# Sliding-window attention with a dropless expert layer on one core: when the first expert tiles are closed, and which engine issues which load and store

## The chip, the cores and the metric

The kernel runs on one core of one Trainium2 chip. The metric is the device time of one execution in microseconds (us). Engines are called by their names (TensorE for matrix products, VectorE, ScalarE, GpSimd, SyncE); in the profile's rows they are PE (PEld its weight loads), DVE, ACT, POOL and SP. SPq, ACTq and POOLq are instructions with which those engines issue transfers.

## What is computed

Attention over 8 batch items with 8 heads, 576 positions and head width 64; a position sees itself and the 63 before it. Its output, 4608 tokens of 512 values, goes through a layer of 8 experts, of which each token takes the one with the largest logit.

```python
scores = scale * np.matmul(q, k.transpose(0, 1, 3, 2))
rel = pos[:, None] - pos[None, :]
mask = (rel >= 0) & (rel < 64)
scores = np.where(mask, scores, -1000000000.0)
attn = softmax(scores); out = np.matmul(attn, v)
x = out.transpose(0, 2, 1, 3).reshape(4608, 512)
logits = x @ w_gate                       # 512 x 8
expert_idx = np.argmax(logits, axis=1)
gate_w = softmax(logits)[np.arange(N), expert_idx]
for e in range(8):                        # tokens sorted by expert
    y[e's] = np.maximum(x[e's] @ w1[e], 0.0) @ w2[e]   # 512 x 1024, 1024 x 512
out = gate_w[:, None] * y
```

## The kernel before

**Attention.** Two batch items form a pair (`bg`, 0 to 3) of 1152 tokens, nine blocks of 128 (`NTB`): four whole ones of each item, and a ninth made of the last 64 positions of both (the "rests"). A unit `u` is a pair and two heads; there are 16. Each unit takes three steps (`c` = 0, 1, 2) of three blocks, so there are N = 48 steps, all written out; `step(s)` (L896) issues, in this order for every engine: `scored(s + 1)` (L550, q times k, into banks 0 and 1), `masked` (L578, VectorE) and `softened` (L591, exponentials on ScalarE); `weighted(s - 1)` (L609, times v, into bank 6); `logit(s - 3)` (L648); `flipped(s)` (L598, transposes of the weights; one copy back by VectorE, one by ScalarE); `divided(s - 1)` (L624, VectorE reads bank 6); loads, if the step is a unit's first; `turned(s + 3)` (L522, transposes of q and k, copied back by ScalarE; `c` = 2 turns the rests); `x_turned(s - 2)` (L637); and what stands under `s` in the dictionary `todo`. Each engine does its instructions in the order in which they are written. Before step 0, steps -3 to -1 run their parts: `turned(0)`, `turned(1)`, then `scored(0)` and `turned(2)`.

**Loads.** `load_qk(u)` (L481) issues eight loads of 128 KB for a unit, `load_v(u)` (L505) four, with GpSimd's copies that shift v by half a block; `load_rests(bg)` (L492) six for a pair. All are issued by SyncE, the first ones in the order of L876 to L883: unit 0's q and k, the gate weights `wg`, a zero row, the rests, v, then units 1 and 2.

**Routing.** When a pair's logits are complete, `by_tokens` (L661) and `choose` (L677) find on VectorE each token's expert, its gate weight and its rank among the expert's tokens, in five parts. `after` (L833) spreads them and what follows over the next steps: `place` (L744, two VectorE instructions a block), `weigh` (L751, x times gate weight) and `store` (L759, to `x_dram`).

**Expert tiles.** A tile has 256 slots, in two chunks of 128 tokens (`C` = 2). Tiles 0 and 1 always belong to expert 0 and hold tokens of the first three pairs only, so that they can start before the last pair is routed: after the third pair (`last - 1`), L730 raises expert 0's count to at least 512. `first_tiles` (L857), in the last part of `after` for that pair, writes the tokens of both tiles into `perm_e`: a comparison on VectorE (`hi_e`) and 54 small matmuls (L869). `gather_first` (L277) clears tile 0's rows and fetches them by an indirect load. A tile's work is `hidden` (L314, seven products of a Strassen-like scheme, each some 1.9 us of TensorE in the rows), `turn` (L299, transposes of the next tile, eight, with two copies by ScalarE), `sums_x` (L307, VectorE) and `output` (L367, seven more products). `sums_w2` (L152) forms four sums of w2 on GpSimd.

**Between.** After the last step the code from L939 on interleaves by hand the last attention parts, tile 0 (`next(tile0)` issues one product) and the last pair's routing, whose nine blocks ScalarE weighs in `weigh_some` and SyncE stores. `slot_table` (L779) then makes the table of all other tiles: a comparison (`hi`), `fill` for the first 27 blocks, `place` and `fill` for the last nine. Then come tile 1, expert 0's third tile, and a loop over the experts with branches on the counts (from L1007 on).

Of the kernel before, what the change touches and what calls it, by code (L numbers as in the profile page):

```python
# [20 lines left out]
WINDOW = 64  # L21
# [15 lines left out]
def kernel(  # L37
# [45 lines left out]
    ident = consts.tile([P, P], F32, name="ident")  # L83
    make_identity(nc, ident[:])
    GE = 32
    wg = consts.tile([P, NG, GE], F32, name="wg")
# [125 lines left out]
    key = rt.tile([P, NJE], BF16, name="key")  # L212
    hi_e = rt.tile([P, NJE, NE * C], BF16, name="hi_e")
    at_b = rt.tile([P, NJ], BF16, name="at_b")
# [21 lines left out]
    VW = D + 1  # L236
    ST = 3
    NST = NTB // ST
# [37 lines left out]

    def gather_first(tokens):  # L277

        for c in range(C):
            G.memset(xg[c], 0.0)  # L280

            G.indirect_dma_start(
                out=xg[c], out_offset=None, in_=x_dram[0 : NT - BG * S, :],
                in_offset=bass.IndirectOffsetOnAxis(ap=tokens[:, c : c + 1], axis=0),
                bounds_check=NT - BG * S - 1, oob_is_err=False,
            )
# [11 lines left out]

    def turn():  # L299

        for c in range(C):
            for g in range(NG):
                nc.tensor.transpose(out=tps[c][:, g, :], in_=xg[c][:, g * P : (g + 1) * P], identity=ident[:])  # L303
            nc.scalar.copy(out=xq[:, :, c], in_=tps[c].rearrange("p (a g) s -> p a g s", a=2))
        yield

    def sums_x():  # L307

        b12, b22, b21 = tps[1][:, 0:HG], tps[1][:, HG:], tps[0][:, HG:]
        for n, (a, b) in enumerate(((b12, xq[:, 0, 0]), (b22, xs[:, 0]), (b22, xq[:, 0, 1]), (xs[:, 1], b21))):  # L310
            V.tensor_tensor(out=xs[:, n], in0=a, in1=b, op=ALU.subtract)
# [128 lines left out]
    with tc.manual_schedule(), ExitStack() as held, ExitStack() as brief:  # L440
# [5 lines left out]
        sc_ring, tr_ring = cycle((0, 1)), cycle((2, 3, 4, 5))  # L446


        NM = 2 + ST
        mask = consts.tile([P, NM, P], BF16, name="mask")  # L450
        nc.gpsimd.memset(mask[:], 0.0)
        for h in range(2):
            for m0, m1, first in ((0, 1, False), (1, 2, h == 0), (2, NM, False)):
                rows = slice(h * D, (h + 1) * D)
                sel = partial(
                    nc.gpsimd.affine_select, out=mask[rows, m0:m1, :], in_=mask[rows, m0:m1, :], fill=MASKED,
                )
                if first:
                    sel(pattern=[[0, m1 - m0], [-1, P]], compare_op=ALU.is_ge, base=0, channel_multiplier=1)
                else:  # L460
                    sel(pattern=[[0, m1 - m0], [1, P]], compare_op=ALU.is_gt, base=0, channel_multiplier=-1)
                    sel(pattern=[[0, m1 - m0], [-1, P]], compare_op=ALU.is_ge, base=WINDOW, channel_multiplier=1)
        NVR = 3
# [16 lines left out]

        def load_qk(u):  # L481
            bg, g = units[u]
            qks[u] = [qk_m(((u % 3 + 2) % 3 * 2 + n) * 1024, BG, NV, 2, D) for n in range(2)]
            for i in range(BG):
                for t, src in zip(qks[u], (q, k)):
                    for h in range(2):
                        nc.sync.dma_start(
                            out=t[:, i, :, h, :],
                            in_=src[bg * BG + i, 2 * g + h, 0:SM, :].rearrange("(p j) d -> p j d", j=NV),
                        )  # L490

        def load_rests(bg):  # L492

            at = 6144 + bg % 2 * 2048
            vr = qk_m(at + 1024, BG, H, D)
            rests[bg] = [qk_m(at, H, D), qk_m(at + 512, H, D), vr]
            for t, src in zip(rests[bg], (q, k)):
                for i in range(BG):
                    nc.sync.dma_start(
                        out=t[i * D : (i + 1) * D], in_=src[bg * BG + i, :, SM:S, :].rearrange("h p d -> p h d")  # L500
                    )
            for i in range(BG):
                nc.sync.dma_start(out=vr[D:P, i], in_=v[bg * BG + i, :, SM:S, :].rearrange("h p d -> p h d"))

# [172 lines left out]
        def choose(bg):  # L677
# [49 lines left out]
            V.tensor_tensor(out=count[:], in0=count[:], in1=inc[:, :, NTB - 1], op=ALU.add)  # L727
            if bg == last - 1:

                V.tensor_scalar_max(count[:, 0:1], count[:, 0:1], float(NE * TB))  # L730
            V.tensor_tensor(out=rank[:], in0=rank[:], in1=ranks[:, 1], op=ALU.subtract)
# [47 lines left out]
        def slot_table(hi):  # L779
# [25 lines left out]
            def fill(j):  # L805
                for i in range(2):
                    nc.tensor.matmul(slots, lhsT=lo[:, i, j], rhs=hi[:, j], start=(i + j == 0), stop=(i + j == NJ))

            for j in range(NJE):
                fill(j)  # L810
            for n in range(NST):
                for m in range(ST):
                    place(NJE + n * ST + m)
                yield
            for j in range(NJE, NJ):
# [17 lines left out]
        def after(s, routing, bg):  # L833
# [13 lines left out]

            for n in (0, 0, 1, 2, 2):
                do(n, part)
            for m in range(NTB):  # L850
                do(3 + m // 3, partial(place, bg * NTB + m))
                do((2, 2, 3, 3, 4, 4, 4, 5, 5)[m], partial(weigh, bg, m, nc.scalar if m in (2, 6) else G))
                if m % ST == ST - 1:
                    do(3 + m // ST, partial(store, bg, m // ST, G))
            do(6, first_tiles)

        def first_tiles():  # L857

            V.scalar_tensor_tensor(
                out=key[:], in0=rkhi[:, 0:NJE], scalar=1.0, in1=oh_all[:, 0, 0:NJE], op0=ALU.add, op1=ALU.mult  # L860
            )
            V.tensor_tensor(
                out=hi_e[:], in0=_inner(key[:], NE * C), in1=_ins(hi_id[:, C + 1 : C + 1 + NE * C], 1, NJE),
                op=ALU.is_equal,
            )
            slots = banks[next(tr_ring)](0, NE * C)
            for j in range(NJE):
                for i in range(2):
                    nc.tensor.matmul(  # L869
                        slots, lhsT=lo[:, i, j], rhs=hi_e[:, j], start=(i + j == 0), stop=(i + j == NJE)  # L870
                    )
            V.tensor_scalar(out=perm_e[:], in0=slots, scalar1=-1.0, scalar2=float(NT), op0=ALU.mult, op1=ALU.add)
            gather_first(perm_e[:, 0:C])

        N = NU * NST
        load_qk(0)  # L876
        nc.sync.dma_start(out=wg[:, :, 0:E], in_=moe_w_gate.rearrange("(g p) e -> p g e", p=P))
        nc.sync.dma_start(out=x_dram[NT : NT + 1, :], in_=zrow[:])
        load_rests(0)
        load_v(0)  # L880
        load_qk(1)
        load_v(1)
        load_qk(2)  # L883

# [11 lines left out]
        def step(s):  # L896
            if 0 <= s + 1 < N:
                prs[s + 1] = softened(*masked(s + 1, scored(s + 1)))
# [7 lines left out]
            if s >= 0 and s % NST == 0:  # L906
                u = s // NST
                if u + 3 < NU and (u + 3) % NG == 0:
                    load_rests((u + 3) // NG)
                if u + 2 < NU:  # L910
                    load_v(u + 2)
                if u + 3 < NU:
                    load_qk(u + 3)
            if s + 3 < N:
# [13 lines left out]

        for n, s in enumerate((N - 6, N - 3)):
            fs = slice(n * HF, (n + 1) * HF)  # L930
            todo.setdefault(s, []).append(partial(nc.sync.dma_start, out=w2s[0][:, fs], in_=w2v[0][:, fs]))
        for s in range(-3, N):
            step(s)
        assert not todo
        sums_w2(0)

        tr_ring = cycle((4, 5))  # L939
        tile0 = chain(hidden(0), turn(), output(0))  # L940
        px = weighted(N - 1, pTs.pop(N - 1))
        form_all(turn())
        logit(N - 3)
        divided(N - 1, px)
        x_turned(N - 2)
        sums_x()
        gather_first(perm_e[:, C : 2 * C])
        by_tok = [by_tokens(last, c) for c in range(NST)]
        next(by_tok[0])
        next(tile0)  # L950
        logit(N - 2)
        x_turned(N - 1)
        next(by_tok[0], None)
        next(by_tok[1])
# [21 lines left out]
        weigh_some(1)  # L976
        next(tile0)
        next(routing, None)
        weigh_some(2)
        next(tile0)  # L980
        brief.close()
        hi = held.enter_context(tc.tile_pool(name="hot", bufs=1)).tile([P, NJ, NS], BF16, name="hi")
        table = slot_table(hi)
        for _ in range(8):
            next(tile0)
            next(table, None)
        assert next(tile0, None) is None
        gather(perm_i[:, 3 * C : 4 * C])
# [82 lines left out]
```

## Time and profile before

| | us |
|---|---|
| median of 3 runs (lowest, highest) | 765.39 (765.24, 767.0) |
| the profiled execution | 764.28 |
| its span, first to last instruction | 762.4 |
| TensorE busy | 720.1 (94%) |
| VectorE busy | 395.0 (52%) |
| GpSimd busy | 357.1 (47%) |
| ScalarE busy | 268.4 (35%) |
| mean granted TensorE clock | 0.986 |

Attention takes the first 214 us, tile 0 lasts until about 247 and tile 1 until about 275; the rest are the experts' other tiles. In the profile's rows the first number is the start, the second the duration, in us from the start of the span; then engine, line, operation, output <- inputs, shapes and number. In brackets stands how long the engine sat idle before, and what released it.

### The profile page before, as it was taken

The page shows a single profiled execution, that of the slowest core. Times are in us where ns is not written, and L with a number is a line of the kernel's source. Part 1 is how long each engine was busy: PE and PEld are TensorE (multiplying, and loading weights), DVE is VectorE, ACT ScalarE, POOL GpSimd, SP SyncE. Part 2 cuts the span into 40 slices and gives each one's busy share as a digit, 9 for nine tenths or more (in the row PEclk, how much of TensorE's full clock was granted, in tenths as well). Part 3 has the DMA queues.
Part 4 walks back from the last instruction along what each step waited for, and adds up shares of the span by engine and source line. Part 5 has one row for each costly group of instructions (what it writes and reads, how often), then busy time and mean ns, then how long its engine had stood idle before and what let it go on. Part 6 is the DMA issues. An engine that isn't in the chain of part 4 may idle for free. (4 is left out here: it accounts for less than half of the span.)

```text
span 762.4 us, 18401 instructions
## 1 busy us (share of the span) xinstructions
PE 720.1 (94%) x7018; PEld 650.5 (85%) x7018; DVE 395.0 (52%) x1355; ACT 268.4 (35%) x676; POOL 357.1 (47%) x366
## 2 busy tenths in 40 slices
PE   4999999999899999999999999999999999999995
PEld 3888888887688988998999899899988899988994
DVE  2677997988758544523542353352434452424432
ACT  4888888887543201211121122011220121211220
POOL 5215558593860635537531653663266465262111
PEclk8999999999899999999999999999999999999998
DMA  8997889983513712604410360542171171101101
GB/s 162 226 205 173 175 181 255 213 225 113 195 42 126 277 58 67 229 29 138 159 56 30 96 208 30 166 142 70 31 257 45 40 254 56 43 24 42 43 29 54
DMA packets 137620, 94.55 MB, mean 124 GB/s; under 512 B 117072, under 2 KB 117072, under 8 KB 137490
## 3 DMA queue, kind: packets, MB, share of 16 engines
q1 hardware_dynamic: 127858, 62.16, 29.8%
q0 software_dynamic: 9056, 28.58, 11.7%
q10 hardware_dynamic: 576, 2.10, 0.8%
q8 instruction: 78, 1.28, 0.7%
q14 instruction: 52, 0.43, 0.2%
HBM read 73.94 MB, written 20.45 MB: 124 GB/s over the span
## 5 line engine op out<-in xcount | busy, mean ns | idle before, releaser
L322 PE MATMUL bank<-qk_m,s 128*128 128x128 f32 x1216 | 145.4, 275 | 0.0
L322 PEld LDWEIGHTS bank<-qk_m,s 128*128 128x128 f32 x1216 | 140.4, 192 | 0.0
L322 PE MATMUL bank<-qk_m,w 128*128 128x128 f32 x912 | 112.2, 276 | 12.5 <-DVE v_m L358 8.8
L272 POOL DMA_INDIRECT qk_m<-x_dram,at_g x42 | 44.6, 1063 | 167.5 <-PE bank L303 160.2
L322 PEld LDWEIGHTS bank<-qk_m,w 128*128 128x128 f32 x912 | 106.7, 192 | 17.5 <-issue 17.3
L595 ACT ACTIVATE pr<-pr,mx 128x128 f32<-128x128 f32 x288 | 89.7, 390 | 31.8 <-DVE mx L585 31.5
L358 DVE TENSOR_TENSOR v_m<-bank,v_m 128x256 f32<-128x256 f32 x101 | 40.8, 422 | 110.1 <-PE bank L362 54.8
L585 DVE CUSTOM_DVE_ANT_0 pr<-bank,mask 128x128 f32<-128x128 f32 x288 | 64.4, 286 | 27.7 <-PE bank L572 26.1
L329 ACT COPY qk_m<-bank 128x512 f32<-128x512 f32 x19 | 11.2, 587 | 165.7 <-PE bank L322 155.2
L292 POOL DMA_INDIRECT out_dram<-v_m,at_s x42 | 42.4, 1010 | 56.5 <-DVE v_m L358 44.7
L139 POOL TENSOR_TENSOR s<-w 128x1024 f32<-128x1024 f32 x22 | 52.3, 2376 | 19.1 <-DMA qk_m<-x_dram,at_g 14.8
L362 PE MATMUL bank<-qkT_m,v_m 128*128 128x256 f32 x240 | 54.0, 380 | 1.7 <-DVE v_m L139 1.7
L362 PEld LDWEIGHTS bank<-qkT_m,v_m 128*128 128x128 f32 x240 | 45.4, 190 | 8.5 <-DVE v_m L139 2.5
L362 PE MATMUL bank<-qk_m 128*128 128x256 f32 x224 | 52.1, 380 | 0.0
L513 POOL COPY v_m<-v_m 64x520 f32<-64x520 f32 x32 | 19.8, 618 | 67.0 <-DMA v_m<-in_v_dram 59.7
L618 PEld LDWEIGHTS bank<-v_m,pT 128*64 128x64 f32 x1152 | 40.5, 139 | 11.6 <-DVE xs L632 5.8
L618 PE MATMUL bank<-v_m,pT 128*64 128x65 f32 x1152 | 47.2, 229 | 2.6 <-DVE xs L632 2.6
L362 PE MATMUL bank<-s,v_m 128*128 128x256 f32 x216 | 48.1, 379 | 0.0
L362 PEld LDWEIGHTS bank<-qk_m 128*128 128x128 f32 x224 | 41.5, 190 | 5.5 <-ACT v_m L374 0.4
L362 PEld LDWEIGHTS bank<-s,v_m 128*128 128x128 f32 x216 | 41.0, 190 | 5.6
L572 PE MATMUL bank<-qkT_m 64*64 64x128 f32 x1152 | 44.8, 286 | 0.1
L539 PE MATMUL bank<-ident,qk_m 128*128 128x128 f32 x256 | 36.6, 287 | 8.7 <-DMA qk_m<-in_q_dram 8.1
(167 smaller groups left out, 1220.7 us busy)
## 6 DMA issues: line engine op xcount, KB each, us to landing
w<-in_moe_w_dram SPq DMA_DIRECT2D x11, 2048.0 KB, 9.2
qk_m<-in_q_dram SPq DMA_DIRECT2D x72, 128.0 KB, 3.8
qk_m<-in_k_dram SPq DMA_DIRECT2D x72, 128.0 KB, 3.7
v_m<-in_v_dram SPq DMA_DIRECT2D x64, 128.0 KB, 3.7
qk_m<-in_moe_w_dram SPq DMA_DIRECT2D x3, 2048.0 KB, 16.1
x_dram<-xs POOLq DMA_DIRECT2D x6, 512.0 KB, 4.8
x_dram<-xs POOLq DMA_DIRECT2D x3, 768.0 KB, 5.3
w<-in_moe_w_dram ACTq DMA_DIRECT2D x4, 512.0 KB, 5.0
```

The costliest lines, as they stand in the source:

```text
L139: op()
L272: G.indirect_dma_start(out=xg[c], out_offset=None, in_=x_dram[:, :], in_offset=bass.IndirectOffsetOnAxis(ap=at_g[:, c : c + 1], axis=0),)
L292: put = G.indirect_dma_start(out=out[:, :], out_offset=bass.IndirectOffsetOnAxis(ap=at_s[:, c : c + 1], axis=0), in_=ys[c], in_offset=None ...
L322: nc.tensor.matmul(acc[:, f, :], lhsT=a[:, g, f * P : (f + 1) * P], rhs=b[:, g, :], start=(first and f == 0 and g == 0), stop=(g == HG - 1 ...
L358: plus = lambda out, a, b: V.tensor_tensor(out=out, in0=a, in1=b, op=ALU.add)
L362: nc.tensor.matmul(acc, lhsT=a[:, f, :], rhs=b[:, f, :], start=(start and f == 0), stop=(stop and f == HF - 1), skip_group_check=True,)
L513: nc.gpsimd.tensor_copy(out=vb[0:D, i].rearrange("p j h d -> p (j h d)"), in_=va[D:P, i].rearrange("p j h d -> p (j h d)"),)
L539: nc.tensor.transpose(out=tr.rearrange("d a b -> d (a b)").rearrange("d (p j) -> d j p", j=NV)[:, j, :], in_=t[:, c, j].rearrange("p h d - ...
L572: nc.tensor.matmul(out_, lhsT=qT[rows, t, a * WINDOW : (a + 1) * WINDOW], rhs=rhs, start=True, stop=True, skip_group_check=True,)
L585: V.tensor_tensor_reduce(out=prs[h][:, m, :], in0=scs[h][:, m, :], in1=mask[:, m0 + m, :], scale=-scale, scalar=-2 * MASKED, op0=ALU.add, ...
L595: nc.scalar.activation(out=y, in_=y, func=AF.Exp, scale=-1.0, bias=mx[:, h, m : m + 1])
L618: nc.tensor.matmul(px[a * D : (a + 1) * D, h, m, :], lhsT=pTs[h][:, m, a * D : (a + 1) * D], rhs=vt[:, h, :], start=True, stop=True, skip_ ...
```

## The change

- Expert 0's count is raised to 256 after the second pair and to 512 after the third. Tile 0 is filled from the first two pairs and tile 1 from the first three, each by its own `first_tile`: comparison first, then the small matmuls (36 for tile 0, 54 for tile 1, two columns wide instead of four) and the gather. Tile 0's comparison stands in step N-10, its matmuls and gather in N-9; tile 1's behind the last step.
- Tile 0's transposes and `sums_x` move into step N-2 (into banks 0 and 1), its first product and `sums_w2` into step N-1; the loads of w2 one step earlier.
- For the third pair, `choose`, `place` and `weigh` get other steps; GpSimd weighs all nine blocks (before: seven, ScalarE two), and SyncE stores instead of GpSimd.
- In the table, the fill of 27 blocks comes after the second three of the last places, and the last `weigh_some` comes later.
- The masks are made first on GpSimd. The rests of the first two heads are loaded by ScalarE, followed by the gate weights; v and unit 1 follow unit 0 directly on SyncE; the other heads' rests are loaded by GpSimd.
- `scored(0)` stands between `turned(0)` and `turned(1)`; ScalarE's exponentials for it come after `turned(1)`'s copies, and `turned(2)` comes in step 0.

The core of the diff (the move of the mask code, with its text unchanged, and the signatures are left out):

```diff
-            if bg == last - 1:
-                V.tensor_scalar_max(count[:, 0:1], count[:, 0:1], float(NE * TB))
+            if last - NE <= bg < last:
+                V.tensor_scalar_max(count[:, 0:1], count[:, 0:1], float((bg - last + NE + 1) * TB))
...
-            for j in range(NJE):
-                fill(j)
             for n in range(NST):
                 for m in range(ST):
                     place(NJE + n * ST + m)
+                if n == 1:
+                    for j in range(NJE):
+                        fill(j)
                 yield
...
-            for n in (0, 0, 1, 2, 2):
+            for n in (0, 1, 1, 2, 3):
                 do(n, part)
             for m in range(NTB):
-                do(3 + m // 3, partial(place, bg * NTB + m))
-                do((2, 2, 3, 3, 4, 4, 4, 5, 5)[m], partial(weigh, bg, m, nc.scalar if m in (2, 6) else G))
+                do((4, 4, 5, 5, 6, 6, 7, 7, 7)[m], partial(place, bg * NTB + m))
+                do((2, 3, 3, 4, 4, 5, 5, 6, 6)[m], partial(weigh, bg, m, G))
                 if m % ST == ST - 1:
-                    do(3 + m // ST, partial(store, bg, m // ST, G))
-            do(6, first_tiles)
-
-        def first_tiles():
+                    do(4 + m // ST, partial(store, bg, m // ST, nc.sync))
+        def first_tile(n):
+            nj = (last - NE + n + 1) * NTB
...
-            gather_first(perm_e[:, 0:C])
+            to = perm_e[:, n * C : (n + 1) * C]
+            V.tensor_scalar(out=to, in0=slots, scalar1=-1.0, scalar2=float(NT), op0=ALU.mult, op1=ALU.add)
+            gather_first(to, nj * P)
+            yield
...
-        load_qk(0)
-        nc.sync.dma_start(out=wg[:, :, 0:E], in_=moe_w_gate.rearrange("(g p) e -> p g e", p=P))
-        nc.sync.dma_start(out=x_dram[NT : NT + 1, :], in_=zrow[:])
-        load_rests(0)
-        load_v(0)
-        load_qk(1)
+        load_qk(0, nc.sync, nc.sync)
+        load_rests(0, 0, 2, nc.scalar)
+        load_v(0)
+        load_qk(1, nc.sync, nc.sync)
+        load_rests(0, 2, H, G)
+        nc.scalar.dma_start(out=wg[:, :, 0:E], in_=moe_w_gate.rearrange("(g p) e -> p g e", p=P))
+        nc.sync.dma_start(out=x_dram[NT : NT + 1, :], in_=zrow[:])
         load_v(1)
-        load_qk(2)
+        load_qk(2, nc.sync, nc.sync)
...
-        for n, s in enumerate((N - 6, N - 3)):
+        for n, s in enumerate((N - 7, N - 4)):
...
-        for s in range(-3, N):
+        tile0 = chain(hidden(0), turn(), output(0))
+        first = first_tile(0)
+        todo.setdefault(N - 10, []).append(partial(next, first))
+        todo.setdefault(N - 9, []).append(partial(next, first))
+        free = [banks[i](0, NG, P) for i in (0, 1)]
+        todo.setdefault(N - 2, []).extend((lambda: form_all(turn(free)), partial(sums_x, free)))
+        todo.setdefault(N - 1, []).extend((partial(next, tile0), partial(sums_w2, 0)))
+        turned(0)
+        first = masked(0, scored(0))
+        turned(1)
+        prs[0] = softened(*first)
+        for s in range(N):
             step(s)
-        sums_w2(0)
-        tile0 = chain(hidden(0), turn(), output(0))
         px = weighted(N - 1, pTs.pop(N - 1))
-        form_all(turn())
         logit(N - 3)
         divided(N - 1, px)
         x_turned(N - 2)
-        sums_x()
-        gather_first(perm_e[:, C : 2 * C])
+        second = first_tile(1)
+        next(second)
+        next(tile0)
         by_tok = [by_tokens(last, c) for c in range(NST)]
         next(by_tok[0])
-        next(tile0)
         logit(N - 2)
         x_turned(N - 1)
+        next(second)
...
         weigh_some(1)
-        next(tile0)
         next(routing, None)
-        weigh_some(2)
         next(tile0)
...
-        for _ in range(8):
+        for n in range(8):
             next(tile0)
             next(table, None)
+            if n == 1:
+                weigh_some(2)
```

## The prediction

> **What bounds the kernel now.** First the page: TensorE is busy for 94% of the span, so only the 42 us in which it is not can be won without taking matmuls away.
>
> ```profile
> PE 720.1 (94%) x7018; PEld 650.5 (85%) x7018; DVE 395.0 (52%) x1355; ACT 268.4 (35%) x676; POOL 357.1 (47%) x366
> ```
>
> Second the waits of TensorE over the whole span (total, times, longest), for the names of the gaps.
>
> ```profile
> PE bank L322 <- DVE v_m L358: 8.8, 8, 1.4
> PE bank L539 <- DMA qk_m<-in_q_dram: 8.1, 3, 4.9
> ...
> PE bank L869 <- DVE hi_e L862: 2.7, 1, 2.7
> PE bank L618 <- DVE xs L632: 2.6, 6, 0.9
> ...
> PE bank L643 <- DVE pT L605: 1.4, 1, 1.4
> PE bank L807 <- DVE qk_m L311: 1.3, 1, 1.3
> ```
>
> The first row (expert changes) is not touched. The second is the start, the other four lie between 187 and 240 us, where attention ends and tile 0 begins. Nothing waits in between (between 30 and 180 us the list has 1.4 us). So there are two places. Third, the start in order of time (start, duration, engine, [idle before]):
>
> ```profile
> 0.81 1.28 ACT L544 ACT_TABLE_LOAD   x1 [0.81 <-PEq L1057]
> ...
> 9.69 1.56 PE L572 MATMUL bank<-qkT_m 64*64 64x128 f32 x24
> ...
> 18.32 2.28 PE L539 MATMUL bank<-ident,qk_m 128*128 128x128 f32 x8 [2.88 <-DMA qk_m<-in_q_dram]
> 24.39 0.89 PE L572 MATMUL bank<-qkT_m 64*64 64x128 f32 x24
> ```
>
> The reader sees ScalarE's table load at the very start (the first transposes follow at 4.94), `scored(0)` at 9.69, a wait for unit 1's q before 18.32, and `scored(3)` at 24.39, from where TensorE hardly stops. Fourth, the other place, and then TensorE's clock there by the microsecond (length, busy by engine, granted clock, DMA):
>
> ```profile
> 187.11 0.55 PE L643 MATMUL bank<-ident,xs 128*128 128x128 f32 x3 [1.41 <-DVE pT L605]
> ...
> 202.13 1.56 PE L869 MATMUL bank<-hi_e,lo 128*128 128x4 bf16 x54 [2.70 <-DVE hi_e L862]
> ```
> ```profile
> 202.00:203.00 1.00, 0.87 (x34) 0.87 (x34) 0.08 (x1) 0.22 (x1) 1.00 (x3) 0.72 0.64 180
> ...
> 205.00:206.00 1.00, 1.00 (x20) 0.89 (x17) 0.76 (x7) 0.37 (x2) 0.00 (x0) 0.50 0.02 8
> ...
> 209.00:210.00 1.00, 0.73 (x12) 0.34 (x12) 0.59 (x2) 0.84 (x2) 0.97 (x2) 0.86 0.34 90
> ```
>
> `first_tiles` stands in VectorE's queue behind a whole step's softmax work, so TensorE idles 2.70 us, and then works at clock 0.50 until 209.1.
>
> **The start.** VectorE, GpSimd and TensorE get no new work; the order of loads decides. What goes: 5.2 us of SyncE between unit 0's last k (issued until 6.22) and its v (11.46), in which it issued the gate weights, the zero row and six rests. Unit 1's q would then be issued near 9.9 and land near 13.2 (issue to landing 3.0 to 3.4 us on the first loads), 5 us ahead of 18.3: that 2.88 us wait goes. What is late next is ScalarE. In the built program the hardware loads of SyncE and ScalarE take eight completion semaphores in turn, and a ninth waits until the first user of its semaphore has landed. SyncE's fourth load (second k) so waits for ScalarE's first rest load. No row shows such a load; its neighbours are the gate load's 2.4 us and the q loads' 2.6 (least), 3.6 (median) and 6.1 (most); I take 2.8, the small ones, so it goes out at 3.6 instead of 2.90. The last q of unit 0 waits for the second q (landed 4.94): out at 5.0 (before 4.24), landed at 8.0. The gate load stands on ScalarE ahead of its table load and first copy, and waits for just that landing (and for GpSimd's `wg` memset, now behind the masks: masks from 1.9, 4.3 us long, so 6.5). Hence 8.1, + 0.55 issue, + 1.28 table load = 9.95; two copies of 0.59 with their gaps and the hand-over to TensorE: `scored(0)` at 11.4, 1.7 us later than before.
>
> From there, with the rows' durations: `scored(0)` 1.56 and `turned(1)` 2.04, both at the slow pace of the first rows, to 15.0; ScalarE's last copy ends at 15.65; its order has both softmaxes after the four copies, 2 x 1.86 to 19.4; copies of 0.46, 0.37 and two of 0.59 to 21.4. TensorE needs the 0.37 one for `scored(2)` (done 20.5), then 0.97 + 0.87 + 1.04 for `weighted(0)`, `flipped(1)`, `turned(4)`: `scored(3)` at 23.2 against 24.39. **Start: -1.2 us.** Ends: if the gate load did not hold ScalarE, `scored(0)` would come at 7.7, 3.7 us sooner: -4.9. If small loads land in 6.1, the same chain puts `scored(0)` at 17.6: +5.0.
>
> [...]
>
> GpSimd's six loads come after its copies for unit 0 (v landed near 12.2, so from 13.5). Nearest rows are its stores, 0.56 to 0.82 us each: issued by 18.4, landed by 22. Unit 1's `turned(5)` comes near 25.5, so nothing waits; each microsecond past that would be TensorE's. Behind them on GpSimd wait unit 1's v copies, used only by `weighted(3)`, still later.
>
> **The end of attention.** Stalls of the old chain, per row: 0.24 before the ranks (L705), 1.41, a `scored` stretched from 0.89 to 1.43 (0.54), 0.48, 2.70, the slow clock, 0.27, 0.88, and 1.29 before the table's fill (L807). The slow clock: from 203.63 the five groups of that step start 1.48, 1.55, 0.58, 1.34 and 0.83 apart, and 0.81, 0.90, 0.35, 0.71 and 0.48 apart at full clock: 2.53. Sum 10.34.
>
> Added: 36 small matmuls with their weights in step N-9; the 54 of L869 took 1.56, so 1.0 us on TensorE. The other 54 stay, two columns wide. Key and `hi_e` come a step earlier, so no wait. VectorE in that step waits for the 36 before `perm_e`, then has the next `scored` anyway.
>
> Left or new stalls, from VectorE's queue (per step: six masks 1.27, pT 0.55, `divided` 0.9, against 3.2 to 4.1 of TensorE):
> - Ranks now follow `oh` in the same step: `oh` would end at 178.5, TensorE is there at 178.06: 0.5.
> - The chain of `choose` is cut in two of 1.3 us, in separate steps; the 1.41 goes.
> - Places: two tiles a step in three steps, 0.45 us a tile alone, 0.8 beside GpSimd's weighing (six instructions in 2.41 us at 191.82). GpSimd weighs nine at 1.57 without pause, from about 181 to 195, so two of these steps are dear: the lag passes VectorE's slack by 0.3 and 0.7.
> - Step N-1: VectorE has `sums_x` (1.65) and three places (1.35, dear 2.4) before pT and `divided`, which `weighted(N-1)` needs: 0.1 + 0.8. ScalarE's two copies and TensorE's eight transposes of tile 0 only move forward, into the 0.27 and 0.88.
> - The table: TensorE does one hidden part more before the last logit and one output part more before the fill, so it comes there as soon as before. VectorE's chain loses 0.69 (ScalarE's third weighing stood before the relu that L139 needs), 0.91 and one add of 0.6; then the last fill waits for the last places: 1.1 in all instead of 1.29.
>
> Sum 3.5. SyncE's stores (six issues, 4.9 us in the last pair) delay only the second w2 half, queued behind the first store: weighed by 187, loaded in 6.0, used after 197. Without that cover GpSimd's four sums (9.5 us) and tile 1's gather behind them slip, and that gather has 4 us before tile 1's transposes. **End: -10.34 + 1.0 + 3.5 = -5.8 us**, between -8 (hardly a new stall) and -2.4 (they double).
>
> [...]
>
> **Sum.** The profiled execution is 764.28 (span 762.4), 1.1 below the median of the runs, 765.39. 764.28 - 1.2 - 5.8 = 757.3; toward the median I say 757.5.
>
> **Rivals.**
> 1. The start wins in full (-4.9): 764.28 - 4.9 - 5.8 = 753.6. For: SyncE's 5.2 us do go. Against: ScalarE's order. 0.12.
> 2. Stalls move into VectorE's last steps: -1.2 - 2.4: 760.7. For: VectorE was 99% busy from 190 to 200. Against: work is spread over three more steps. 0.18.
> 3. Slower: the shared semaphores hold SyncE's fourth load and then ScalarE's queue at every landing, `scored(0)` at 17.6: 764.28 + 5.0 - 2.4 = 766.9. It decides once `scored(0)` is later than 17.3 with the weak end, 20.7 with the forecast one. Against: the first q landed 3.4 us after issue. 0.07.
> 4. The closing does not do what it says: expert 0 short of 256 tokens in the first two pairs, so that slots stay empty. Counted from the reference's seeded inputs it has 265 and 538 tokens after two and three pairs, so the number of tiles stays at 19 full and 2 half. No chance; but gain and loss cancelling otherwise, near 764: 0.03.
>
> The forecast has 0.60. The range 753.5 to 762.5 leaves out 3 and 4 and the outer half of 1. No change is within 0.3% (2.3 us, about what a measurement of this kernel can tell): faster 0.60 + 0.12 + 0.18 less 0.02 of 2's tail = 0.88, same 0.05, slower 0.07.
>
> **What would show it.** Right: in the new profile ScalarE's table load near 8.7 instead of 0.81, `scored(0)` near 11.4, `scored(3)` near 23; no wait at the small matmuls, clock 1.00 throughout the end of attention, and waits for VectorE there of 3 to 4 us in all. Wrong: `scored(0)` before 9 or after 14, a wait at unit 1's `turned(5)`, a clock of 0.50 after 190 us, or waits on expert rows that were not there.

## The result, and the profile after

| | us |
|---|---|
| before, median of 4 | 765.36 (765.24 to 767.0) |
| after, median of 4 | 770.31 (769.55 to 770.45) |
| ratio | 1.0058, 95% interval 1.004 to 1.0075 |
| after, the profiled execution | 770.18, span 768.2 (before 764.28, span 762.4) |
| predicted | 757.5 (753.5 to 762.5) |

The change makes the kernel 5 us slower; 8 us faster was forecast. All medians and ratios here are of fast executions; the only slow one, at 778.28 us, was of x8_no_pause and is left out. To see where the time went, the two traces are read at the same points of the work: the start of `scored(s)` of certain steps s, and T, the start of the transposes in the middle of tile 1's work (they are of expert 0's third tile; at 259.69 us before, 265.13 after). The first row is the time up to a point, the others from point to point:

| us | to scored(3) | to scored(13) | to scored(38) | to scored(43) | to T | to the end |
|---|---|---|---|---|---|---|
| before | 24.39 | 38.33 | 99.21 | 19.96 | 77.80 | 502.7 |
| after | 22.66 | 40.35 | 99.34 | 21.52 | 81.26 | 503.1 |
| difference | -1.73 | +2.02 | +0.1 | +1.56 | +3.46 | +0.4 |

So the start gained what was forecast, and a little more, and lost it within ten steps, and the end of attention, which should have given 5.8, took 5.0 (1.56 + 3.46). The page of after, and the waits of TensorE over its whole span (total, times, longest):

```profile
PE 721.2 (94%) x7054; PEld 650.8 (85%) x7054; DVE 406.0 (53%) x1359; ACT 265.6 (35%) x674; POOL 360.2 (47%) x368
```
```profile
PE bank L644 <- DVE pT L606: 4.2, 3, 2.2
...
PE bank L573 <- DVE mx L586: 3.1, 4, 2.3
PE bank L619 <- DVE xs L633: 2.6, 5, 0.6
PE bank L619 <- ACT pT L606: 1.6, 1, 1.6
```

VectorE is busy 406.0 us instead of 395.0, with four instructions more. That is the first hint: its instructions have become longer. The waits at `hi_e` and at the table's fill are gone from the list; in their place TensorE waits for VectorE's ordinary softmax work (pT, mx).

The start, and step 6 (start, duration, engine, [idle before]; ACTq is ScalarE's issue of a load):

```profile
9.01 1.28 ACT L545 ACT_TABLE_LOAD   x1 [9.01 <-DMA qk_m<-in_q_dram]
11.43 1.56 PE L573 MATMUL bank<-qkT_m 64*64 64x128 f32 x24 [3.56 <-ACT qkT_m L545]
...
29.93 0.34 ACTq L928 DMA_DIRECT2D w<-in_moe_w_dram  x1
30.31 1.86 ACT L596 ACTIVATE pr<-pr,mx 128x128 f32<-128x128 f32 x6 [3.45 <-DMA qk_m<-in_k_dram]
```

`scored(0)` is at 11.43 and `scored(3)` at 22.66, as forecast. At 29.93 ScalarE issues its second w1 load, late: ScalarE does no other work for 3.45 us, until a load of k has landed, which w1 has nothing to do with. The trace holds the reason: this issue waits for semaphore 107, the completion semaphore (it tells that a load has landed) which SyncE's k load of 25.04 used last. That load lands at 29.91, and w1 goes out 0.02 us later. The exponentials behind it wait as well, and `scored(6)` comes 6.48 us after `scored(5)`, instead of 4.07. In the kernel before, the load that the second w1 load has to wait for had landed 1.9 us earlier (25.69 against 27.57).

The end of attention: VectorE's instructions, GpSimd beside them, TensorE's waits, and one microsecond's row (length, busy by engine, then the granted clock, 0.50, the DMA share and GB/s):

```profile
191.18 0.29 DVE L738 TENSOR_REDUCE r_pos<-r_rank 128x9 int32<-128x72 f32 x1
...
192.00 0.79 DVE L741 CAST rkhi<-r_half 128x9 f32<-128x9 int32 x1
196.70 2.24 DVE L747 TENSOR_SCALAR lo<-lane,low,tok_a 128x128 bf16<-128x128 bf16 x1
203.49 2.39 DVE L747 TENSOR_SCALAR lo<-lane,low,tok_b 128x128 bf16<-128x128 bf16 x1
```
```profile
182.66 13.90 POOL L758 TENSOR_SCALAR xs<-xs,gate 128x512 f32<-128x512 f32 x9
196.53 2.35 POOL L156 TENSOR_TENSOR qkT_m<-qk_m 128x1024 f32<-128x1024 f32 x1
203.48 2.35 POOL L156 TENSOR_TENSOR qkT_m<-qk_m 128x1024 f32<-128x1024 f32 x1
```
```profile
189.86 0.55 PE L644 MATMUL bank<-ident,xs 128*128 128x128 f32 x3 [2.18 <-DVE pT L606]
195.95 0.55 PE L644 MATMUL bank<-ident,xs 128*128 128x128 f32 x3 [1.80 <-DVE pT L606]
207.00 0.43 PE L573 MATMUL bank<-qkT_m 64*64 64x128 f32 x2 [2.27 <-DVE mx L586]
```
```profile
210.00:211.00 1.00, 1.00 (x13) 0.50 (x10) 1.00 (x1) 0.00 (x0) 1.00 (x1) 0.50 0.09 25
```

The cast of 128 x 9 numbers takes 0.79 us beside the weighing, and half a place takes 2.24 or 2.39: it begins while one of GpSimd's sums of w2 runs and ends 0.05 or 0.06 us after it. The reduction next to the cast keeps its 0.29. In the kernel before the same work looked like this, first VectorE, then GpSimd:

```profile
184.75 0.17 DVE L740 CAST rkhi<-r_half 128x9 f32<-128x9 int32 x1
187.86 0.31 DVE L746 TENSOR_SCALAR lo<-lane,low,tok_a 128x128 bf16<-128x128 bf16 x1
```
```profile
190.35 0.82 POOL L766 DMA_DIRECT2D x_dram<-xs  x1 [8.08 <-issue]
```

GpSimd stood still for 8.08 us there: its first store waited until ScalarE had weighed m = 2. VectorE's choosing and its first places (182.6 to 189.2) fell into that pause. The change gave all nine weighings to GpSimd and the stores to SyncE, and so removed the pause.

### The profile page after: what moved, and what is told of

It reads as the page before. It is cut to its first block, busy times and chain, and to the rows that moved or that the text cites. A ratio compares the mean times of both kernels' runs of the same rounds, so it can differ in the third digit from the quotient of the medians.

```text
span 768.2 us, 18502 instructions
## 1 busy us (share of the span) xinstructions
PE 721.2 (94%) x7054; PEld 650.8 (85%) x7054; DVE 406.0 (53%) x1359; ACT 265.6 (35%) x674; POOL 360.2 (47%) x368
## 3 DMA queue, kind: packets, MB, share of 16 engines
q10 hardware_dynamic: 1968, 2.31, 1.1%
## 5 line engine op out<-in xcount | busy, mean ns | idle before, releaser
L573 PEld LDWEIGHTS bank<-qkT_m 64*64 64x64 f32 x1152 | 32.0, 134 | 16.2 <-ACT qkT_m L545 4.5
```

Source lines behind the costliest of these rows:

```text
L573: nc.tensor.matmul(out_, lhsT=qT[rows, t, a * WINDOW : (a + 1) * WINDOW], rhs=rhs, start=True, stop=True, skip_group_check=True,)
```

## The experiments

SBUF operations are here those whose operands lie in SBUF, the memory of the kernel's tiles; softmax, by contrast, mostly reads TensorE's results in PSUM (`bank` in the rows). Theory: **(a)** GpSimd's long SBUF operations, when they run beside VectorE's small SBUF operations, stretch those, and TensorE waits; **(b)** the start's gain is real and is lost because ScalarE's second w1 load waits for a completion semaphore that a load of SyncE still holds. Rivals: the closing itself costs; VectorE's order of work is to blame, not GpSimd; transfers are the limit, whoever issues them. Each run has its ratio to the kernel before on the same chip; where a trace is read, it is of one execution. Code lines are shortened.

### x1_start_only: the change's start, all else of before

> The kernel before with the new start alone (masks first, loads in order of use by three engines, shared prologue); everything after the start is of before. Theory (two separate effects: the start gains 1.7 to 2 us, but ScalarE's second load of w1 waits for a completion semaphore that it shares with a q or k load of SyncE, and gives it back at step 6; the loss lies at the end of attention): scored(3) near 22.7, the wait near 30 us for exponentials again, and 765.4 within 0.8 us. Rival A (the start keeps its gain, and the whole loss is at the end): 763.4 to 763.7. Rival B (the start delays GpSimd or the loads lastingly, and the end only shows it): 768 or more.

765.78, ratio 0.999 (0.9977 to 1.0004). `scored(3)` at 23.02 (-1.37), then +2.4 up to `scored(13)` with a wait for exponentials of 1.4 us; from `scored(43)` to T 77.29 us (before 77.80), and from there to the end as before. The start is worth nothing here, and does not cause the loss at the end: rival B falls.

### x2_old_schedule: the closing with the third pair's steps and engines of before

```
-            for n in (0, 1, 1, 2, 3):                    +            for n in (0, 0, 1, 2, 2):
-  do((4, 4, 5, 5, 6, 6, 7, 7, 7)[m], place ...)          +  do(3 + m // 3, place ...)
-  do((2, 3, 3, 4, 4, 5, 5, 6, 6)[m], weigh, G)           +  do((2, 2, 3, 3, 4, 4, 4, 5, 5)[m], weigh, ACT if m in (2, 6) else G)
-  do(4 + m // ST, store, SyncE)                          +  do(3 + m // ST, store, G)
```

> The kernel after, with the third pair's choosing, placing, weighing and storing in the steps and on the engines of the kernel before (ScalarE weighs two of nine, GpSimd stores). Theory (GpSimd's unbroken weighing, and its w2 sums behind it, run beside VectorE's small SBUF operations and stretch them tenfold; the pause of GpSimd in before sheltered them): the pause returns, places at 0.17 to 0.4 us again for the most part, waits of TensorE on pT and masks under 3 us in all, and 760 to 763. Rival (the closing itself costs: 36 fills, tile 0's work moved forward into attention): 769 to 771.

764.26, ratio 0.9975 (0.996 to 0.999): 6 us under after. The pause is back (6.80 us) and with it the short cast:

```profile
185.90 0.17 DVE L741 CAST rkhi<-r_half 128x9 f32<-128x9 int32 x1
...
191.53 0.87 POOL L767 DMA_DIRECT2D x_dram<-xs  x1 [6.80 <-ACT pr L596]
```

From `scored(43)` to T it needs 72.98 us instead of 81.26 (before 77.80). The closing does not cost; the third pair's new steps and engines do. The median is above the 760 to 763 that were expected; the trace is of the fastest of ten executions.

### x8_no_pause: the steps of x2, but all weighing on GpSimd and stores on SyncE

```
-  weigh(bg, m, ACT if m in (2, 6) else G)     +  weigh(bg, m, G)
-  store(bg, c, G)                             +  store(bg, c, SyncE)
```

> As x2_old_schedule (764.26), but all nine weighings on GpSimd and the stores on SyncE, as in the kernel after; the steps of choosing and placing stay those of before. Theory (what sheltered VectorE was GpSimd's pause, which came from its store waiting for ScalarE's weighing): GpSimd weighs without a pause from about 182 to 196, choose operations at 0.4 to 0.8 us, the sums of w2 from 196 on beside the last places at 2.2 to 2.4 us each, and 768 to 771. Rival (the steps in which choosing and placing stand matter, not GpSimd): 763.5 to 765.5.

769.84, ratio 1.0049 (1.0019 to 1.0079). The executions spread from 765.82 to 775.17, and the traced one is the fastest; even it takes 76.68 us from `scored(43)` to T, 3.7 more than x2. Against x2 only the engines that weigh and store differ, and without the pause the gain is gone, as theory (a) has it:

```profile
189.24 0.79 DVE L741 CAST rkhi<-r_half 128x9 f32<-128x9 int32 x1
...
193.19 0.90 PE L644 MATMUL bank<-ident,xs 128*128 128x128 f32 x3 [5.17 <-DVE pT L606]
```

One detail of the expectation missed: only the first w2 sum ran early here, and of the last places it held one half, for 0.65 us. The cost was one wait of 5.17 us behind choosing, and a half clock until 197.2.

### x3_w2_late: after, with the w2 halves loaded in steps N-2 and N-1

```
-        for n, s in enumerate((N - 7, N - 4)):   +        for n, s in enumerate((N - 2, N - 1)):
```

> The kernel after, with the two halves of expert 0's w2 loaded five and three steps later (N-2 and N-1), so that GpSimd's sums of w2 begin only after attention's places are done. Theory (the sums beside the places stretch each place to 2.3 us): places of tiles 6 to 8 at 0.3 us, the 2.27 wait and the slow clock behind it gone, 766 to 767.5; unless the later sums hold tile 1's gather, then up to 1 us worse. Rival (VectorE's queue order, not GpSimd, delays the places): 769.5 to 771.

770.0, ratio 1.0045 (1.0023 to 1.0067): the number is the rival's, the trace the theory's. The places of blocks 2 to 5 are back at 0.31, and the collision has moved with the sums to the places of the last step, of which three halves take 2.34, 2.38 and 2.84:

```profile
212.68 2.38 DVE L747 TENSOR_SCALAR lo<-lane,low,tok_b 128x128 bf16<-128x128 bf16 x1
...
218.99 1.62 PE L619 MATMUL bank<-v_m,pT 128*64 128x65 f32 x24 [6.76 <-DVE xs L633]
```

### x4_no_weigh: after, without the weighing of the third pair

```
-                do((2, 3, 3, 4, 4, 5, 5, 6, 6)[m], partial(weigh, bg, m, G))
```

> The kernel after without the weighing of the third pair's token rows (nine multiplications by the gate are left out, all else stays). Theory (weighing beside choose stretches VectorE's SBUF operations): choose operations at 0.17 to 0.27 instead of 0.46 to 0.79 us, the waits of 2.18 and 1.80 gone, 765 to 767.5 - less only if the w2 sums, now earlier, leave the places alone. Rival (the choose chain is late for its own order of work): both waits stay and 769.5 to 771.

766.56, ratio 1.0009 (0.9983 to 1.0034). The first half of choosing is at 0.17 to 0.3. In the second half the cast met the single sum that GpSimd ran between 189.96 and 192.36; the operation in front of it, begun 0.01 us after the sum, and those behind it kept 0.17:

```profile
190.17 2.21 DVE L741 CAST rkhi<-r_half 128x9 f32<-128x9 int32 x1
192.42 0.17 DVE L742 TENSOR_SCALAR r_half<-r_pos 128x9 int32<-128x9 int32 x1
```

So a wait of 1.7 us stayed, and one of 3.0 came where two places met the later sums (2.18 and 2.38). From `scored(43)` to T: 76.50, 4.8 less than after.

### x10_pause_in_after: after, with weighings 2 and 6 on ScalarE and the stores on GpSimd

> The kernel after with two of the nine weighings (2 and 6) on ScalarE and the stores on GpSimd as in before; choosing, placing and weighing stay in the steps of after. Theory (the pause matters): GpSimd's store waits for ScalarE's weighing, so it stands still between its second and third weighing for 5 us or more; the first half of choose at 0.17 to 0.3 us and one of the waits of 2.18 and 1.80 gone, the sums of w2 a few us later and so less beside the places: 765 to 768. Rival (steps matter): 769.5 to 771.

768.78, ratio 1.0041 (1.0024 to 1.0058). The pause (5.4 us) removed the 2.18 and the 1.80; then the places of step N-1, which only the new schedule has there, met the w2 sums at 1.25, 2.38 and 2.84, and TensorE waited 5.74 us. Pause and steps are one matter: what counts is which operations meet.

### x9_closing_only: before, with the closing alone

This is x2_old_schedule with the start of before put back.

> The kernel before with the closing of tiles 0 and 1 alone, tile 0's work moved forward as in the change, and the w2 halves one step earlier; start, choosing, placing, weighing and storing of before. Theory (the closing does what was forecast of it; the start's gain and loss cancel): as x2_old_schedule, 763.5 to 765.5, the profiled execution 3 us under that of before, no 2.70 wait and no clock of 0.50 after 200 us. Rival (the start's part is what x2 gains): 766 to 767.

764.23, ratio 0.9987 (0.9964 to 1.0009). `scored(43)` to T takes 73.52; the 2.70 wait is gone and the clock is 1.00 from 180 us to T. The closing gives 4.3 to 4.8 us there and costs 1.4 between `scored(38)` and `scored(43)`: net 2.9 to 3.4 up to T, in the traces of x9 and x2. From T to the end these traces lose 1.3 and 0.7 of it, for a reason that no run looked for, and both are of their kernel's fastest execution. The ratios say 1 to 2 us, and that of x9 alone is not clear of no gain.

### x7_old_sched_w1_sync: x2, with the w1 loads issued by SyncE

```
-  partial(nc.scalar.dma_start, out=w1s[0] ...)   +  partial(nc.sync.dma_start, out=w1s[0] ...)
```

> The kernel after with the third pair's steps and engines of before (as in x2_old_schedule, 764.26), and with expert 0's four w1 loads issued by SyncE instead of ScalarE. Theory (ScalarE's second w1 load waits for a completion semaphore that a q or k load of SyncE still holds, so the next exponentials and TensorE wait, and in some executions the clock falls to 0.50 behind that gap): the wait of weighted on ACT pT near 30 us is gone, scored(8) near 41.5 instead of 43.33, and 760 to 762, with less spread between runs. Rival (the transfers themselves are the limit there, whoever issues): a wait of TensorE on a load of q, k or v takes its place and the time stays within 1 us of 764.3.

764.64, ratio 0.9982 (0.9968 to 0.9995): no gain over x2. Yet the wait at step 6 is gone, and `scored(8)` is at 41.46 instead of 43.33: theory (b) holds for that wait. The 1.9 us, and more, went again between 60 and 90 us, in two ways: unit 5's q and k came late (0.94 and 0.29), so the rival has a part, and GpSimd's last sum of w1 now met the first pair's choosing, with waits of 0.73 and 1.13:

```profile
84.18 2.36 DVE L696 TENSOR_TENSOR oh_all<-e_m,r_idx 128x72 bf16<-128x72 f32 x1
```
```profile
84.09 2.36 POOL L928 TENSOR_TENSOR s<-w,s 128x1024 f32<-128x1024 f32 x1
```

### x11_sums_early: x7, with the w1 sums ahead of unit 5's v copies

```
-            todo.setdefault(3 * NST + n, []).append(op)   +            todo.setdefault(3 * NST - 1, []).append(op)
```

> x7_old_sched_w1_sync (764.64: old steps of the third pair, w1 loads issued by SyncE) with GpSimd's four sums of w1 issued one step earlier, ahead of unit 5's v copies instead of behind them, so that they no longer run beside the first pair's choosing. In x7 those sums ran from 73.8 to 86.4 us and oh_all took 2.36 us beside them instead of 0.23. Theory (GpSimd's long SBUF operations stretch VectorE's small SBUF operations wherever they meet): sums near 60 to 70 us, oh_all at 0.23, the waits of 0.73 and 1.13 at 83 to 89 us gone, the wait for unit 5's q (0.94 and 0.29) stays, and 762 to 763.2. Rival (those waits come from the late loads): 764 to 765.

762.0, ratio 0.994 (0.9916 to 0.9965): faster than both kernels. The sums now run from 63.6 to 73.0, beside VectorE's softmax work, most of which reads PSUM, and nothing is stretched (masks 0.28 to 0.29); `oh_all` is back at 0.23 us. `scored(13)` is at 60.90 (before 62.72): here most of the start's gain lasts. Once more beside x15:

> The same kernel as x11_sums_early once more, beside x15_split_in_pause on one chip: 761 to 763, a ratio of 0.992 to 0.997 to the kernel before. If its gain was of that one chip, 764 or more.

763.39, ratio 0.9962 (0.9944 to 0.9981).

### x12_w1_later: x2, with ScalarE's w1 loads one unit later and the early sums

```
-            step = NST * (g // 2) + g % 2 + 1   +            step = NST * (g // 2 + 1) + g % 2 + 1
```

> x2_old_schedule (764.26) with ScalarE's w1 loads one unit later (steps 4, 5, 7 and 8 instead of 1, 2, 4 and 5), when fewer loads are under way, and the sums of w1 ahead of unit 5's v copies. Theory (only the second load, at 29.5 us, met a completion semaphore still taken by SyncE's q and k loads; the transfers of the first 65 us fit once w1 comes later): no wait of weighted on ACT pT near 30 us, scored(8) near 41.5, no wait of more than 0.5 us from there to 180, and 761.5 to 763. Rival (ScalarE's loads meet SyncE's wherever they stand): a wait on exponentials of 1 us or more reappears at 36 to 55 us, 764 or more.

763.81, ratio 0.996 (0.9936 to 0.9984). The rival was right: ScalarE's loads wait wherever they were put among SyncE's, each until the load that last used its semaphore has landed (0.02 us before the issue, in all four). Behind three of the four the exponentials come late, by 1.74, 2.24 and 2.58 us, for instance (a load of k is named, not of w1):

```profile
54.89 1.87 ACT L596 ACTIVATE pr<-pr,mx 128x128 f32<-128x128 f32 x6 [2.58 <-DMA qk_m<-in_k_dram]
```

An engine on the path should issue no load there.

### x13_split, x14_split_sheltered, x15_split_in_pause: the cut of choosing, sheltered

x13 is x12 with the change's cut of choosing, places in steps 4 to 6 and a longer pause:

```
-  for n in (0, 0, 1, 2, 2):                       +  for n in (0, 0, 1, 2, 3):
-  do(3 + m // 3, place)                           +  do(4 + m // 3, place)
-  do((2, 2, 3, 3, 4, 4, 4, 5, 5)[m], weigh)       +  do((2, 2, 4, 4, 5, 5, 5, 6, 6)[m], weigh)
-  do(3 + m // ST, store)                          +  do(4 + m // ST, store)
```

x14 is x11 with these lines, and tile 1's `key` and `hi_e` in step N-2; x15 is x14 with them in step N-5.

> x12_w1_later with the third pair's choosing cut as in the change (the last part a step later), the places in steps 4 to 6, and ScalarE's first weighing two steps after GpSimd's second, so that GpSimd stands still over the whole of choosing. Theory (with VectorE sheltered, the cut brings what was forecast of it): the wait of 1.46 us at 188 us gone, choose at 0.17 to 0.3 us, places at 0.3 to 0.75 us, and 1 us less than x12_w1_later: 760.5 to 762. Rival (the later weighing moves the w2 sums and tile 1's gather onto the path): a wait for the gather near 226 us and 763 or more.

> x11_sums_early (762.0) with the third pair's steps of x13_split, and with tile 1's key and hi_e formed in step N-2, ahead of the sums of x, and so before GpSimd's sums of w2 begin. In x13 the cut won 3.7 us up to scored(47), and then hi_e took 2.31 us beside those sums (0.22 alone), TensorE waited 0.96, and its next sixteen products took 3.45 instead of 1.98. Theory (what is left of the loss is where VectorE's small SBUF operations meet GpSimd's): key and hi_e at 0.2 to 0.6 us, no wait at the 54 fills, no clock under 1.00 behind 190 us, and 758.5 to 760.5. Rival (the w2 sums, now running to 215 us, or the later weighing cost the same): 762 to 764.

> x14_split_sheltered (766.4) with tile 1's key and hi_e formed in step N-5 instead of N-2: at about 193 us, where GpSimd stands still between 186.6 and 195.6. In x14 hi_e met GpSimd's store issues and first w2 sum and took 3.31 us; the product behind it started 2.53 late and ran at half clock. Theory (collisions are the whole of the loss): key and hi_e at 0.2 to 0.3 us, the wait of 2.53 gone, clock 1.00 from 180 to 260, sixteen products in 2.0 us, and 759.5 to 761.5, 1 to 2 us under x11_sums_early. Rival (the later weighing and sums cost in themselves, or the cut brings nothing): a new wait between 205 and 240 us, and 763 or more.

x13: 764.06, ratio 0.9963 (0.9939 to 0.9987). x14: 766.4, ratio 0.9994 (0.9974 to 1.0015). x15: 761.91, ratio 0.9943 (0.9917 to 0.997). In x13 TensorE no longer waits for choosing (2.94 in x12), and from `scored(43)` to `scored(47)` it needs 15.6 us instead of 20.4 (x12's choosing began beside two weighings, so the longer pause has a part in this). Then `hi_e` met a w2 sum (2.31 us), and TensorE's next products ran at half clock. The remedy in x14 put it in front of the first sum, where it ran through two store issues of GpSimd and then the sum, which was worse. Why it did not end before the sum began is open: beside such issues it takes 0.20 to 0.27 in seven other traces. In the pause it costs 0.22. One line of each, in this order, of x13, x14 and x15:

```profile
215.05 2.31 DVE L864 TENSOR_TENSOR hi_e<-key,hi_id 128x54 bf16<-128x54 bf16 x1
```
```profile
207.08 3.31 DVE L864 TENSOR_TENSOR hi_e<-key,hi_id 128x54 bf16<-128x54 bf16 x1
```
```profile
191.82 0.22 DVE L864 TENSOR_TENSOR hi_e<-key,hi_id 128x54 bf16<-128x54 bf16 x1
```

From `scored(43)` to T: 75.34, 78.24 and 73.50. So one operation in the wrong place is worth 4.7 us in the traces (0.5% in the ratios); but with no such collision the cut (73.50) is no better than no cut (72.93 to 74.31 in x2, x7, x9 and both traces of x11; 75.41 in x12). x15's 1 to 2 us over x11 are not shown: 761.91 against 763.39 on the same chip, but their ratios' intervals overlap, and the trace of x11 beside it is the faster (759.88).

## Why the prediction was wrong, step by step

- **The start, -1.2.** Right for what it covered: -1.73 at `scored(3)`, by the order forecast, ScalarE's table load at 9.01 (8.7 forecast) and `scored(0)` at 11.43 (11.4). (The durations that it lists from `scored(2)` on add up to 23.4, not 23.2; it was 22.66.) It stopped at `scored(3)`. The mechanism that it names, completion semaphores shared by SyncE and ScalarE, is in the trace of after: their loads take eight (100, 102 to 108), and SyncE's second k goes out at 3.90, 0.02 us after the landing of ScalarE's first rest, which used its semaphore 100. It acted again at ScalarE's second w1 load, 7 us behind `scored(3)`: 2.41 lost between `scored(5)` and `scored(6)`. Shown by the semaphore that this issue waits for in the trace, by x1 (it comes with the start alone), x7 (gone when SyncE issues) and x12 (back with other loads of ScalarE). Rival 3 had the mechanism, and placed it at `scored(0)`. What the earlier loads could win was then limited by later loads (x7: 1.2 us at unit 5).
- **The 36 fills, +1.0.** Right: 1.04, and the ranks wait 0.48 (0.5 forecast).
- **The 54 fills and the table.** Right: no wait at either, 4.0 us of the old stalls; a new one of 0.46 at the last pair's ranks was not forecast. The last fill of 18 takes 1.53 instead of 0.69, a part of the 1.1 that was left for it.
- **The cut of choosing ("the 1.41 goes").** The step that failed first. It was costed as two chains of 1.3 us, the durations of the old trace, and those were of a sheltered chain. Beside GpSimd's weighing most of its operations take 0.46 to 0.79 instead of 0.17 to 0.29, each half takes 3.5 us, and one wait of 1.41 became two of 2.18 and 1.80. Shown by x2 and x8, which differ only in who weighs and stores, and by x4.
- **The places (0.45 a tile alone, 0.8 beside weighing; 1.0 and 0.9 in sum).** The dear price was right for what it named, and was put on the wrong neighbour: behind the weighing the w2 sums began at 196.53, in attention. The prediction only asked that the second w2 half should not be late, never what an early sum would collide with; it had even written that GpSimd weighs "without pause". Four halves of places met sums, at 2.24, 1.43, 2.39 and 2.28 us instead of 0.31: 7.1 us more on VectorE, of which TensorE saw 2.27 and some smaller waits.
- **The clock at 1.00.** Wrong: 0.50 from 209.5 to 212.9 us, behind these waits. The old trace's 2.53 was also a long case: with the same wait (2.72) x1 has 0.50 for 3.41 us, half as long as before, and the same groups of products lose about 1.5.
- **The end in sum, -5.8.** It measured +5.0. In the traces in which GpSimd's pause shelters choosing and no sum meets a place it is about -3 (x9 -2.9, x2 and x15 -3.4), so some 2.4 us of the forecast were not there in any case: in x15 the waits left are 4.1 us instead of 3.0 behind the ranks, the last fill takes 0.8 more, and about half a microsecond stays unexplained.
- **The rivals.** Rival 2 (stalls move into VectorE's last steps) was the right kind, with a price of 3.4 us where 10.8 came. No rival had VectorE's own instructions getting longer.

The rows show how far the stretch goes. Halves of places that began early in a sum of 2.35 us took 2.2 to 2.4 instead of 0.31; beside weighings the reduction kept its 0.29, and the masks (their inputs are PSUM and the mask) took 0.28 to 0.29 beside weighings here and beside sums in x11_sums_early. Beside weighings of 1.55 us each no operation took longer than 1.03 (x12_w1_later), so none was held for a whole one. What holds VectorE is not seen in any trace; that the stretch follows GpSimd's operation is shown.

## What to carry to other kernels

A duration read from a trace is the duration beside what ran on the other engines at that moment: before moving work, note what stood still beside it, and ask what the mover's engine will do with the time that it gets free. A pause that looks like a fault (GpSimd's 8 us) can be what keeps the engine that feeds the critical one fast, so work off the path is placed by what it collides with, not as early as it can be. And an engine whose work the critical one waits for should not issue loads while others' loads are under way: in these runs ScalarE waited for landings that were not its own.

## What the runs showed of the hardware

- Casts, places, `oh_all` and `hi_e` on VectorE, of 0.17 to 0.31 us each alone, took 2.2 to 2.4 where they began early in a GpSimd sum of 128 x 1024 (2.35 us), to within 0.1 us of its end. Two took 2.84, through the clear (0.5 us) that followed the sum at once (x3_w2_late, x10_pause_in_after), and one 3.31 (x14_split_sheltered).
- In every trace, away from the end of the span, TensorE's stretches at clock 0.50 last 3.41 or 6.83 us, whatever the gap before them. All eight gaps of 2.5 us or more after the start had such a stretch beginning within them or up to 2 us behind them; below that, length did not decide. TensorE idled 2.01 us in x9_closing_only and kept 1.00; it idled 1.99 us in x11_sums_early and went to 0.50 1.5 us later, for 3.41 us; in x13_split a gap of 0.96 us, the longest there, was followed by one. First x9, then x11, each with a microsecond's row (the clock stands behind the engines):

```profile
188.67 0.55 PE L642 MATMUL bank<-ident,xs 128*128 128x128 f32 x3 [2.01 <-DVE pT L604]
190.00:191.00 1.00, 1.00 (x32) 0.93 (x30) 1.00 (x7) 1.00 (x3) 0.00 (x0) 1.00 0.00 0
```
```profile
186.09 0.55 PE L644 MATMUL bank<-ident,xs 128*128 128x128 f32 x3 [1.99 <-DVE pT L606]
188.00:189.00 1.00, 1.00 (x19) 0.86 (x19) 1.00 (x9) 1.00 (x4) 0.00 (x0) 0.50 0.00 0
```

  The longer length is twice the shorter. What decides below 2.5 us, and whether it has a part in the spread of single kernels here (3 to 9 us, 759.67 to 765.16 in x11_sums_early), no run tested.
